# Sums of V and K rows in a decode step with its gradients: 64 one-column matmuls against 16 wide ones in column strips

## The chip, the cores and the metric

The kernel runs on one core of one Trainium2 chip. The metric is the device time of one execution in microseconds (us); the time of a kernel is the median over its runs. Engines are named as the profile names them: PE is TensorE's matmul and PEld its weight load, DVE is VectorE, ACT is ScalarE, POOL is GpSimd, SP is SyncE.

## What is computed

One token's residual step, x + attention + gated MLP on a layer-normed x, and its gradients with respect to x, the K and V caches and all weights. There are 32 heads, each with its own K and V cache of 8192 rows of 128 in bf16, so a cache of a head is 2 MB. Cut to attention:

```python
q = (xn @ wq) per head
scores = einsum("bhqd,bhkd->bhqk", q, k) * (Dh ** -0.5)
p = softmax(scores)
o = einsum("bhqk,bhkd->bhqd", p, v)
out = x + o_of_all_heads @ wo + mlp(xn)
# gradients, with do = the part of grad_out @ wo.T that belongs to the head
#   dv[k,:] = p[k] * do                  dp[k] = do . v[k,:]
#   u[k]    = p[k] * (dp[k] - sum(p*dp))
#   dk[k,:] = u[k] * scale * q           dq = scale * sum_k u[k] * k[k,:]
#   dwq, dwo, dx follow from dq, o and xn
```

Nearly all bytes are the caches read (2 x 64 MB) and the gradients dk and dv written (2 x 64 MB).

## The kernel before, in words

Setup (L102 to L665) loads and differentiates the MLP, while the first K and V tiles arrive. Then one loop over the heads (L691 to L741) follows, and a last head and an end (L743 on). All five engines' orders are written out by hand: an engine runs its instructions in the order of the program text, and each waits where its data aren't there yet.

A head's cache tile is 128 partitions x 64 row groups (j) x 128 columns (`Kt`, `Vt`). In the loop `c` is the current head and `n` the next. The next head's scores and its products with V are computed while the current head's gradients are written. For one head the steps are:

- `product` (L381): VectorE multiplies half the columns of K by q (or of V by do) into a tile `T` (L395), and TensorE adds these up with eight matmuls by the identity, of 512 moving columns each (L397), into the PSUM bank `psS` or `psDP`. Two halves make one product.
- `row_max` (L436): VectorE sums the bank into `S_sb` (L438) and takes the maximum (L440); TensorE brings the maxima of all partitions together (L442). `exps` (L445): VectorE's `negM` (L447), ScalarE's Exp (L450), TensorE's total (L451). `probs` (L453): VectorE's `rZ` (L455) and `P2` (L457), every probability twice, in bf16.
- `attend` (L462): o, the sum over rows of p times V. For each of the 64 row groups TensorE loads the group's 128x128 block of V as weights and multiplies it with one column of `P2`; all 64 add up in column 0 of the bank `ob` (L465).
- `row_dots` (L470) and `dscores` (L478): VectorE sums `psDP` (L472), its dot with P (L475), TensorE's total (L476), VectorE's `U2` (L480) and `Uf` (L485). Then dq in the same way as o: 64 weight loads of K blocks, 64 one-column matmuls into column 1 of `ob` (L487).
- `outer` (L400): dv and dk, half a head at a time, into `ot`: VectorE makes 24 of 32 row groups (L417), ScalarE eight (L411). A finished `ot` of 2 MB is stored by POOL's DMA queue (L424). Loads of K and V go by SP's queue (L112, L119).
- `turn_wq` and `keep_wq` (L490, L495) turn the head's part of wq. `weights` (L499): VectorE scales the two sums into `odq` (L502) and copies dq as bf16 (L504); ScalarE makes `dq_diag` (L506) and `om` (L510); TensorE spreads dq (L508), puts o in place for dwo (L513, a product with 32 weight columns whose output starts at partition 0, 32, 64 or 96) and adds to dx (L516). `keep_dq` (L519) keeps the spread dq.
- Once in four heads `prep_steps` (L271) prepares q and do for the next group of four, with copies `woT` by ScalarE (L288), and `finish_steps` (L335) writes dwo and, once in two groups, the columns of dwq. `gap()` places one such step at a time.

The columns of dwq that are done are stored in two pieces of three and two column blocks (`WQ_PARTS`, L428), both by `sparing` (L141): this splits a transfer of 128 partitions in 120 and 8 rows, and with small pad transfers into `lane_pad` (L134) sets which of the 16 DMA engines gets less of it.

In the loop VectorE's order around a head's end is: T of V second half (n), `odq` and `odq_bf` (c), T of K first half of the head after. TensorE's is: psDP second half (n), then `weights(c)`, then psS first half of the head after.

Of the kernel before, what the change touches and what calls it, by code (L numbers as in the profile page):

```python
# [9 lines left out]
BF16 = mybir.dt.bfloat16  # L10
F32 = mybir.dt.float32
ALU = mybir.AluOpType
ACTF = mybir.ActivationFunctionType
AX = mybir.AxisListType
PSUM = bass.MemoryType.PSUM

P = 128
# [4 lines left out]
def kernel(  # L22
# [22 lines left out]
    nc = tc.nc  # L45
# [16 lines left out]
    NB = NF + 1  # L62
    ACT_J = 8
    TAIL = 2
    LANES = 16
    SPARED = 4
    assert H % GW == 0 and GW % GH == 0 and 0 < REST < P and P % GH == 0
# [32 lines left out]
    with tc.manual_schedule(engines=ORDERED):  # L100
# [119 lines left out]
        DXN0 = 0  # L220
        OUT0 = NC
        OP0 = 16

        sel = consts.tile([P, P // GH], F32, name="sel")
        nc.vector.tensor_reduce(sel[:], ident_f[:].rearrange("p (q r) -> p q r", r=GH), AX.X, ALU.add)
        rmask = consts.tile([P, GH], F32, name="rmask")
        nc.vector.tensor_reduce(rmask[:], ident_f[:].rearrange("p (q r) -> p r q", r=GH), AX.X, ALU.add)

# [42 lines left out]
        def prep_steps(g):  # L271
            G_ = grp[g]
            wq_g, wo_g = G_["wq"], G_["wo"]

            def bank(name, dt, pool=None, tag="w"):
                if g == 0 and pool is not None:
                    return pool.tile([P, GH * DH], dt, name=name, tag=tag)
                return ps_w.tile([P, GH * DH], dt, name=name, tag="w")

            def turn(ci):  # L280
                ps_t = bank("ps_t", BF16, ps_o, "ob")
                for hh in range(GH):
                    nc.tensor.transpose(ps_t[:, hh * DH:(hh + 1) * DH], wo_g[:, hh, ci * P:(ci + 1) * P], ident_bf[:])  # L283
                return ps_t

            def keep(ps_t):
                woT = wpool.tile([P, GH * DH], BF16, name="woT", tag="woT", bufs=2)
                nc.scalar.copy(woT[:], ps_t[:])  # L288
                return woT

            ps_q = bank("ps_q", F32, ps_s, "sm")
            for ci in range(NC):
                nc.tensor.matmul(ps_q[:], lhsT=xn_col_bf[:, ci:ci + 1].to_broadcast([P, P]), rhs=wq_g[:, ci, :],
                                 start=(ci == 0), stop=(ci == NC - 1))
            yield
            qs_g = wpool.tile([P, GH, DH], BF16, name="qs_g", tag="qs_g")
            nc.scalar.activation(qs_g[:].rearrange("p h d -> p (h d)"), ps_q[:], ACTF.Copy, scale=scale)
            G_["qs"] = qs_g
            ps_t = turn(0)
            yield  # L300
            woT = keep(ps_t)
            ps_t = turn(1)
            yield
            ps_d = bank("ps_d", F32, ps_acc, "acc")
            for ci in range(NC):
                nc.tensor.matmul(ps_d[:], lhsT=g_col_bf[:, ci:ci + 1].to_broadcast([P, P]), rhs=woT[:], start=(ci == 0), stop=(ci == NC - 1))
                if ci + 1 < NC:
                    woT = keep(ps_t)
                if ci + 2 < NC:
                    ps_t = turn(ci + 2)  # L310
                if ci not in (2, NC - 1):
                    yield
            do_g = wpool.tile([P, GH, DH], BF16, name="do_g", tag="do_g")
            nc.scalar.copy(do_g[:].rearrange("p h d -> p (h d)").rearrange("p (q r) -> p r q", r=GH),  # L314
                           ps_d[:].rearrange("p (r q) -> p r q", r=GH))
            G_["do"] = do_g
# [108 lines left out]
                if columns:  # L425
                    store_columns()

        WQ_PARTS = ((0, 3), (3, 2))  # L428
        columns = []

        def store_columns():
            b, c0, n = columns.pop(0)
            part, _, dst = wq_part(b, c0, n)
            store(dst, part, by=sparing)

        def row_max(st):  # L436
            st.S = small.tile([P, J], F32, name="S_sb", bufs=1)
# [15 lines left out]
        def probs(st):  # L453
# [5 lines left out]
            nc.scalar.activation(st.Pf[:], st.E[:].rearrange("p (a j) -> p a j", a=2)[:, :, JH - ACT_J:JH],  # L459
                                 ACTF.Copy, scale=rZ[:])  # L460

        def attend(st):  # L462
            st.ob = ps_o.tile([P, 512], F32, name="ob", tag="ob")
            for j in range(J):
                nc.tensor.matmul(st.ob[:, 0:1], lhsT=st.V[:, j, :], rhs=st.P2[:, j, 0:1], start=(j == 0),  # L465
                                 stop=(j == J - 1), skip_group_check=True)
            while behind_o:
                on_sums(*behind_o.pop(0))

        def row_dots(st):  # L470
            st.DP = small.tile([P, J], F32, name="DP_sb", bufs=1)
            nc.vector.tensor_reduce(st.DP[:], st.ps["DP"][:], AX.X, ALU.add)  # L472
            rdot = small.tile([P, 1], F32, name="rdot")
            junk = small.tile([P, J], F32, name="junk", bufs=1)
            nc.vector.scalar_tensor_tensor(junk[:], st.DP[:], 1.0, st.P2[:, :, 0], ALU.mult, ALU.mult, accum_out=rdot[:])  # L475
            nc.tensor.matmul(st.sm[:, 4:5], lhsT=ones_f, rhs=rdot[:], start=True, stop=True, skip_group_check=True)  # L476

        def dscores(st):  # L478
            st.U2 = small.tile([P, J, 2], BF16, name="U2", bufs=1)
            nc.vector.scalar_tensor_tensor(st.U2[:], st.DP[:].unsqueeze(2).to_broadcast([P, J, 2]), st.sm[:, 4:5], st.P2[:],  # L480
                                           ALU.subtract, ALU.mult)
            st.Uf = None
            if st.h < H - 1:
                st.Uf = small.tile([P, 2, ACT_J], F32, name="Uf")
                nc.vector.tensor_copy(st.Uf[:], st.U2[:, :, 0].rearrange("p (a j) -> p a j", a=2)[:, :, JH - ACT_J:JH])  # L485
            for j in range(J):
                nc.tensor.matmul(st.ob[:, 1:2], lhsT=st.K[:, j, :], rhs=st.U2[:, j, 0:1], start=(j == 0), stop=(j == J - 1),  # L487
                                 skip_group_check=True)

        def turn_wq(st):  # L490
            st.ps_wqT = ps_w.tile([P, D], BF16, name="ps_wqT", tag="w")
# [6 lines left out]

        def weights(st):  # L499
            G_, hh = st.G, st.hh  # L500
            odq = small.tile([P, 2], F32, name="odq")
            nc.vector.tensor_tensor(odq[:], st.ob[:, 0:2], sc2[:], ALU.mult)  # L502
            odq_bf = small.tile([P, 1], BF16, name="odq_bf")
            nc.vector.tensor_copy(odq_bf[:], odq[:, 1:2])  # L504
            dq_diag = small.tile([P, P], BF16, name="dq_diag", bufs=1)
            nc.scalar.activation(dq_diag[:], ident_bf[:], ACTF.Copy, scale=odq[:, 1:2])  # L506
            st.ps_db = ps_w.tile([P, DH], F32, name="ps_db", tag="w")
            nc.tensor.matmul(st.ps_db[:], lhsT=ones_bf[:], rhs=dq_diag[:], start=True, stop=True)  # L508
            om = small.tile([P, GH], F32, name="om")
            nc.scalar.activation(om[:], rmask[:], ACTF.Copy, scale=odq[:, 0:1])  # L510
            if hh == 0:
                G_["on_ps"] = accbank[:, OP0 + GH * (st.g % 2):OP0 + GH * (st.g % 2 + 1)]
            nc.tensor.matmul(G_["on_ps"][hh * (P // GH):(hh + 1) * (P // GH), :], lhsT=sel[:], rhs=om[:],  # L513
                             start=True, stop=True, skip_group_check=True)
            for ci in range(NC):
                nc.tensor.matmul(accbank[:, DXN0 + ci:DXN0 + ci + 1], lhsT=st.wqT[:, ci * P:(ci + 1) * P],  # L516
                                 rhs=odq_bf[:], start=False, stop=True, skip_group_check=True)
# [75 lines left out]

        sm_f = wpool.tile([P, 9, NB], F32, name="sm_f", tag="dqbc_g", bufs=1)
        gate, up, th, sig, silu, hcol, t1, dgate, dup = (sm_f[:, i, :] for i in range(9))
        dhc = small.tile([P, NB], F32, name="dhc", bufs=1)
        dgu2 = small.tile([P, 2, NB], BF16, name="dgu2", bufs=1)
        hcol_bf = small.tile([P, NB], BF16, name="hcol_bf", bufs=1)
        nc.vector.memset(sm_f[:, 0:2, NF:NB], 0.0)
        dh0 = dh_product(0, W2A)  # L600
        dh1 = dh_product(W2A, W2A)
# [67 lines left out]
        def gap():  # L669
            if steps and next(steps[0], "end") == "end":  # L670
                steps.pop(0)

        first = new_head(0)
        product(first, "S", 0)
        nc.vector.tensor_reduce(dxn_mlp[:], dx_ps[:], AX.X, ALU.add)
# [15 lines left out]
        for h in range(H - 1):  # L691
# [13 lines left out]
            if n:  # L705
                product(n, "S", 1)
            outer(c, c.do, c.P2, c.Pf, "V", h, 1)
            if h + 2 < H:
                load_v(h + 2)
            wq_columns(h, 0)  # L710
# [1 line left out]
                load_wo(g + 1, nc.scalar)  # L712
            gap()
            dscores(c)
            outer(c, c.q, c.U2, c.Uf, "K", h, 0)
            keep_wq(c)
            if n:
                row_max(n)
                product(n, "DP", 0)
# [28 lines left out]
        outer(c, c.do, c.P2, None, "V", H - 1, 0)  # L748
        row_dots(c)
        outer(c, c.do, c.P2, c.Pf, "V", H - 1, 1)  # L750
        keep_dq(prev)
        while steps:
            gap()
        keep_wq(c)
        dscores(c)
        outer(c, c.q, c.U2, None, "K", H - 1, 0)
        weights(c)
        keep_dq(c)
# [33 lines left out]
            nc.sync.dma_start(out_1.rearrange("a b (p c) -> p (a b c)", c=NC), dx_bf[:])  # L792
        ps_fo = ps_w.tile([NC, P], F32, name="ps_o", tag="w")
        nc.tensor.transpose(ps_fo[:], fin[:], ident_f[:])
        fin_bf = consts.tile([NC, P], BF16, name="fin_bf")
        nc.vector.tensor_copy(fin_bf[:], ps_fo[:])
        nc.scalar.dma_start(out_0.rearrange("a b (c p) -> (a b c) p", p=P), fin_bf[:])

# [29 lines left out]
```

## Time and profile before

| | |
|---|---|
| median of three runs | 727.24 us (725.4 to 727.44) |
| the profiled execution's own time | 725.48 us |
| its span, first to last instruction | 723.5 us |
| mean granted TensorE clock | 0.789 of full speed |
| bytes moved by DMA | 303.72 MB, mean 420 GB/s |
| HBM read and written | 151.35 MB and 151.34 MB |
| `odq` (L502) of the first and of the last head | at 77.6 and 700.1 us |

A row of groups names line, engine, operation, output<-inputs, the form, the count, then busy time and mean time of one instruction, then the idle time of the engine just before them and what ended it. Consecutive matmuls overlap, so the busy time of a group is less than its count times the mean. A row of the timeline gives start, duration, engine, line, operation, tiles and count, and in brackets the idle time before it. An fp32 product stands as two weight loads and two matmuls. The granted clock moves between full and half speed within a head: eight psS or psDP matmuls take from 1.89 to 3.6 us.

### The profile page before, as it was taken

How to read it: one execution, taken by the hardware profiler on the slowest of the kernel's cores; microseconds unless marked ns; L12 is line 12 of the kernel's file. 1: busy time of each engine (PE TensorE's matmuls, PEld its weight loads, DVE VectorE, ACT ScalarE, POOL GpSimd, SP SyncE). 2: the span in 40 equal slices, each digit the busy share in tenths (PEclk: the TensorE clock that was granted, in tenths of full speed). 3: DMA queues.
4: the chain of work that ended last, by engine and by line, in shares of the span. 5: the costliest groups of instructions: out<-in, count | busy, mean ns of one | idle time of the engine just before them, and what ended most of it. 6: DMA issues, size and time to landing. Idle time of an engine off the chain costs nothing.

```text
span 723.5 us, 15790 instructions
## 1 busy us (share of the span) xinstructions
PE 555.5 (77%) x6513; PEld 324.3 (45%) x6513; DVE 630.3 (87%) x720; ACT 460.5 (64%) x1391; POOL 55.1 (8%) x98
## 2 busy tenths in 40 slices
PE   5778788778888787887788685778787878787860
PEld 3654444443544454443454342444354435444440
DVE  4789999899989996998899885899799988999990
ACT  2175666786568774785577653786667846787550
POOL 0010000000000210100000200010000000000100
PEclk9698988877877888787687888687788778877775
DMA  9999999999999999999999999999999999999996
GB/s 359 413 415 424 430 430 427 428 427 431 426 431 428 426 424 428 427 412 429 430 427 429 428 427 422 430 411 410 433 425 429 426 432 427 430 429 429 423 424 255
DMA packets 27142, 303.72 MB, mean 420 GB/s; under 512 B 3422, under 2 KB 3494, under 8 KB 9406
## 3 DMA queue, kind: packets, MB, share of 16 engines
q1 hardware_dynamic: 13778, 155.41, 50.9%
q0 software_dynamic: 11552, 139.43, 45.6%
q10 hardware_dynamic: 1740, 7.87, 2.6%
q8 instruction: 51, 0.84, 0.4%
q14 instruction: 21, 0.17, 0.1%
HBM read 151.35 MB, written 151.34 MB: 418 GB/s over the span
## 4 chain that ended last, share of the span: by engine, by line
DMA 42%; DVE 31%; PE 15%; ACT 7%; issue 1%; SPq 0%; POOL 0%; DVEq 0%; ACTq 0%; POOLq 0%
DMA out_dram<-ot 19%; DMA Kt<-in_A_k_cache_dram 15%; DVE T L395 15%; DVE ot L417 10%; PE psS L397 5%; ACT ot L411 4%; DMA lane_pad<-in_A_wq_dram 4%; PE ob L465 2%; DMA out_dram<-wo_g 2%; PE psDP L397 2%; DMA dbc<-in_B_w_dram 2%; DVE S_sb L438 1%; DVE DP_sb L472 1%; PE ob L487 1%; ACT do_g L314 1%
## 5 line engine op out<-in xcount | busy, mean ns | idle before, releaser
L397 PE MATMUL psDP<-T,ident_bf 128*128 128x512 bf16 x512 | 185.8, 529 | 58.7 <-DVE T L395 58.6
L397 PEld LDWEIGHTS <-ident_bf 128*128 128x128 bf16 x1024 | 121.3, 121 | 220.7 <-issue 170.5
L411 ACT ACTIVATE ot<-qs_g,Uf 128x128 bf16<-128x128 bf16 x496 | 151.4, 389 | 58.9 <-DMA out_dram<-wo_g 32.0
L411 ACT ACTIVATE ot<-do_g,Pf 128x128 bf16<-128x128 bf16 x504 | 153.9, 389 | 11.9 <-DMA out_dram<-ot 10.9
L395 DVE TENSOR_TENSOR T<-Kt,qs_g 128x4096 bf16<-128x4096 bf16 x64 | 146.5, 2288 | 16.4 <-DMA Kt<-in_A_k_cache_dram 15.4
L397 PE MATMUL psS<-T,ident_bf 128*128 128x512 bf16 x512 | 148.3, 442 | 6.2 <-DVE T L395 6.1
L395 DVE TENSOR_TENSOR T<-Vt,do_g 128x4096 bf16<-128x4096 bf16 x64 | 146.0, 2281 | 3.9 <-ACT do_g L314 3.7
L417 DVE TENSOR_TENSOR ot<-do_g,P 128x3072 bf16<-128x3072 bf16 (+1 forms) x64 | 112.8, 1763 | 13.7 <-DMA out_dram<-ot 12.7
L417 DVE TENSOR_TENSOR ot<-qs_g,U 128x3072 bf16<-128x3072 bf16 (+1 forms) x64 | 113.2, 1768 | 11.4 <-DMA out_dram<-ot 11.4
L424 POOL DMA_DIRECT2D out_dram<-ot x60 | 32.4, 539 | 534.2 <-DVE Uf L485 275.0
L487 PEld LDWEIGHTS <-Kt 128*128 128x128 bf16 x2048 | 57.5, 97 | 11.6 <-issue 8.9
L487 PE MATMUL ob<-U,Kt 128*128 128x1 bf16 x2048 | 56.8, 164 | 1.7 <-DVE U L480 1.5
L465 PEld LDWEIGHTS <-Vt 128*128 128x128 bf16 x2048 | 56.9, 98 | 0.0
L465 PE MATMUL ob<-P,Vt 128*128 128x1 bf16 x2048 | 56.1, 163 | 0.0
L506 ACT ACTIVATE dq_diag<-ident_bf,odq 128x128 bf16<-128x128 bf16 x32 | 12.8, 400 | 42.3 <-DVE odq L502 42.3
L459 ACT ACTIVATE Pf<-E,rZ 128x16 f32<-128x16 f32 x32 | 9.7, 304 | 45.0 <-DVE rZ L455 40.5
L288 ACT COPY woT<-ps_t 128x512 bf16<-128x512 bf16 x40 | 23.0, 576 | 17.8 <-PE ps_t L283 17.8
L283 PE MATMUL ps_t<-ident_bf,wo_g 128*128 128x128 bf16 x160 | 17.1, 234 | 19.6 <-ACT dqbc_g L523 15.0
L442 PE MATMUL sm<-ident_f,mrow 128*128 128x128 f32 x64 | 17.2, 355 | 18.6 <-DVE mrow L440 18.6
L438 DVE TENSOR_REDUCE S_sb<-psS 128x64 f32<-128x512 f32 x32 | 21.9, 685 | 8.1 <-PE psS L397 8.1
L283 PEld LDWEIGHTS <-wo_g 128*128 128x128 bf16 x160 | 13.6, 106 | 31.6 <-issue 28.4
L476 PE MATMUL sm<-rdot,ones_fc 128*128 128x1 f32 x64 | 11.3, 245 | 18.5 <-DVE junk L475 18.4
(160 smaller groups left out, 508.6 us busy)
## 6 DMA issues: line engine op xcount, KB each, us to landing
out_dram<-ot POOLq DMA_DIRECT2D x60, 2048.0 KB, 27.4
Kt<-in_A_k_cache_dram SPq DMA_DIRECT2D x32, 2048.0 KB, 27.2
Vt<-in_A_v_cache_dram SPq DMA_DIRECT2D x32, 2048.0 KB, 20.5
out_dram<-ot SPq DMA_DIRECT2D x8, 1024.0 KB, 16.5
out_dram<-wo_g ACTq DMA_DIRECT2D x6, 640.0 KB, 15.7
wo_g<-in_A_wo_dram ACTq DMA_DIRECT2D x6, 640.0 KB, 15.5
wq<-in_A_wq_dram SPq DMA_DIRECT2D x2, 1280.0 KB, 20.5
w1t<-in_B_w_dram SPq DMA_DIRECT2D x1, 2160.0 KB, 12.3
```

What stands on the lines that cost most here:

```text
L283: nc.tensor.transpose(ps_t[:, hh * DH:(hh + 1) * DH], wo_g[:, hh, ci * P:(ci + 1) * P], ident_bf[:])
L288: nc.scalar.copy(woT[:], ps_t[:])
L395: nc.vector.tensor_tensor(T[:], src[:, :, ds_], vec[:, ds_].unsqueeze(1).to_broadcast([P, J, DHH]), ALU.mult)
L397: nc.tensor.matmul(ps[:], lhsT=ident_bf[:], rhs=T[:, :, RUN * i:RUN * (i + 1)], start=(half == 0 and i == 0), stop=(half == 1 and i == DHH ...
L411: nc.scalar.activation(st.ot[half][:, JH - ACT_J + j].rearrange("p a b -> p (a b)"), vec, ACTF.Copy, scale=wf[:, half, j:j + 1])
L417: nc.vector.tensor_tensor(st.ot[half][:, 0:n], vec.rearrange("p (a b) -> p a b", b=2).unsqueeze(1).to_broadcast([P, n, DH // 2, 2]), w2[:, ...
L424: nc.gpsimd.dma_start(dst.rearrange("p j d -> p (j d)"), st.rows[:])
L438: nc.vector.tensor_reduce(st.S[:], st.ps["S"][:], AX.X, ALU.add)
L442: nc.tensor.matmul(st.sm[:, 8:8 + P], lhsT=mrow[:].to_broadcast([P, P]), rhs=ident_f[:], start=True, stop=True, skip_group_check=True)
L465: nc.tensor.matmul(st.ob[:, 0:1], lhsT=st.V[:, j, :], rhs=st.P2[:, j, 0:1], start=(j == 0), stop=(j == J - 1), skip_group_check=True)
L487: nc.tensor.matmul(st.ob[:, 1:2], lhsT=st.K[:, j, :], rhs=st.U2[:, j, 0:1], start=(j == 0), stop=(j == J - 1), skip_group_check=True)
L506: nc.scalar.activation(dq_diag[:], ident_bf[:], ACTF.Copy, scale=odq[:, 1:2])
```

## The change

The sums o and dq are made the other way round. Four row groups at a time, the four columns of `P2` (or `U2`) are the weights and the 4 x 128 columns of V (or K) move: 16 matmuls with 4 weight columns and 512 moving columns. Number q writes four partitions from 32 x (q mod 4) on, so the sixteen go round four strips of the array, and each strip adds up four of them. A strip's partition s then holds, in its block s of 128 columns, a part of the sum; the other blocks hold products that aren't wanted. ScalarE copies the whole bank `ob` to SBUF in two halves (`keep_rows`, fp32, in the buffers of `woT`, of which there are now three), and four fp32 matmuls with one moving column (`blocks_sum`) pick block r of the strips with a 0/1 column of `pick` and add up to the column `od`, which `odq` reads in place of `ob`. `ob` is zeroed once, so the 112 partitions that no matmul writes hold zeros.

```diff
+        def wide_sums(src, w2):
+            n = J // WIDE
+            for q in range(n):
+                c0 = STRIP * (q % NS)
+                nc.tensor.matmul(ob[c0:c0 + WIDE, :], lhsT=w2[:, WIDE * q:WIDE * (q + 1), 0],
+                                 rhs=src[:, WIDE * q:WIDE * (q + 1), :].rearrange("p j d -> p (j d)"),
+                                 start=(q < NS), stop=(q >= n - NS), skip_group_check=True)
+        def keep_rows(st):
+            st.wide = []
+            for i in range(2):
+                part = wpool.tile([P, WIDE // 2 * DH], F32, name="wide", tag="woT", bufs=3)
+                nc.scalar.copy(part[:], ob[:, i * (WIDE // 2) * DH:(i + 1) * (WIDE // 2) * DH])
+                st.wide.append(part)
+        def blocks_sum(st, k):
+            c0 = OD0 + 2 * (st.h % 2)
+            st.od = accbank[:, c0:c0 + 2]
+            for r in range(WIDE):
+                i, b = divmod(r, WIDE // 2)
+                nc.tensor.matmul(st.od[:, k:k + 1], lhsT=st.wide[i][:, b * DH:(b + 1) * DH], rhs=pick[:, r:r + 1],
+                                 start=(r == 0), stop=(r == WIDE - 1), skip_group_check=True)
         def attend(st):
-            st.ob = ps_o.tile([P, 512], F32, name="ob", tag="ob")
-            for j in range(J):
-                nc.tensor.matmul(st.ob[:, 0:1], lhsT=st.V[:, j, :], rhs=st.P2[:, j, 0:1], start=(j == 0),
-                                 stop=(j == J - 1), skip_group_check=True)
+            wide_sums(st.V, st.P2)
...
         def dscores(st):
-            for j in range(J):
-                nc.tensor.matmul(st.ob[:, 1:2], lhsT=st.K[:, j, :], rhs=st.U2[:, j, 0:1], start=(j == 0), stop=(j == J - 1),
-                                 skip_group_check=True)
+            wide_sums(st.K, st.U2)
...
         def weights(st):
             G_, hh = st.G, st.hh
+            blocks_sum(st, 1)
             odq = small.tile([P, 2], F32, name="odq")
-            nc.vector.tensor_tensor(odq[:], st.ob[:, 0:2], sc2[:], ALU.mult)
+            nc.vector.tensor_tensor(odq[:], st.od, sc2[:], ALU.mult)
...
+        ob = ps_o.tile([P, 512], F32, name="ob", tag="ob")
+        nc.tensor.matmul(ob[:], lhsT=ident_bf[:], rhs=zero_bf[:].to_broadcast([P, WIDE * DH]), start=True, stop=True)
...
             outer(c, c.do, c.P2, c.Pf, "V", h, 1)
+            keep_rows(c)
...
             dscores(c)
+            blocks_sum(c, 0)
             outer(c, c.q, c.U2, c.Uf, "K", h, 0)
             keep_wq(c)
+            keep_rows(c)
...
```

So `blocks_sum(c, 0)`, for o, stands behind the K sums on TensorE, and `blocks_sum(c, 1)`, for dq, at the head of `weights`, behind psDP's second half. The last head has the same four calls.

Beside this, the second piece of the dwq columns is stored by one plain DMA instead of `sparing`:

```diff
-        WQ_PARTS = ((0, 3), (3, 2))
+        WQ_PARTS = ((0, 3, sparing), (3, 2, nc.gpsimd.dma_start))
```

To make room in SBUF `junk` is written over `S_sb`, and four small tiles of the setup and the end (`dhc`, `dgu2`, `hcol_bf`, `fin_bf`) share buffers with others. `pick` and `zero_bf` are made in the setup.

More of the change, by code (lines that the diff above doesn't have):

```diff
@@ L64 @@
     TAIL = 2
+    STRIP = 32
+    NS = P // STRIP
+    WIDE = 4
     LANES = 16
@@ L222 @@
         OP0 = 16
+        OD0 = 32
         sel = consts.tile([P, P // GH], F32, name="sel")
         nc.vector.tensor_reduce(sel[:], ident_f[:].rearrange("p (q r) -> p q r", r=GH), AX.X, ALU.add)
+        pick = consts.tile([P, WIDE], F32, name="pick")
+        nc.vector.tensor_reduce(pick[:], ident_f[:].rearrange("p (c s) -> p s c", s=STRIP)[:, 0:WIDE, :], AX.X, ALU.add)
+        zero_bf = consts.tile([P, 1], BF16, name="zero_bf")
+        nc.vector.memset(zero_bf[:], 0.0)
         rmask = consts.tile([P, GH], F32, name="rmask")
@@ L286, in keep @@
             def keep(ps_t):
-                woT = wpool.tile([P, GH * DH], BF16, name="woT", tag="woT", bufs=2)
+                woT = wpool.tile([P, GH * DH], BF16, name="woT", tag="woT", bufs=3)
                 nc.scalar.copy(woT[:], ps_t[:])
@@ L426, in outer_v @@
                     store_columns()
-        WQ_PARTS = ((0, 3), (3, 2))
+        WQ_PARTS = ((0, 3, sparing), (3, 2, nc.gpsimd.dma_start))
         columns = []
         def store_columns():
-            b, c0, n = columns.pop(0)
+            b, c0, n, by = columns.pop(0)
             part, _, dst = wq_part(b, c0, n)
-            store(dst, part, by=sparing)
+            store(dst, part, by=by)
         def row_max(st):
@@ L473, in row_dots @@
             rdot = small.tile([P, 1], F32, name="rdot")
-            junk = small.tile([P, J], F32, name="junk", bufs=1)
-            nc.vector.scalar_tensor_tensor(junk[:], st.DP[:], 1.0, st.P2[:, :, 0], ALU.mult, ALU.mult, accum_out=rdot[:])
+            nc.vector.scalar_tensor_tensor(st.S[:], st.DP[:], 1.0, st.P2[:, :, 0], ALU.mult, ALU.mult, accum_out=rdot[:])
             nc.tensor.matmul(st.sm[:, 4:5], lhsT=ones_f, rhs=rdot[:], start=True, stop=True, skip_group_check=True)
@@ L595 @@
         gate, up, th, sig, silu, hcol, t1, dgate, dup = (sm_f[:, i, :] for i in range(9))
-        dhc = small.tile([P, NB], F32, name="dhc", bufs=1)
-        dgu2 = small.tile([P, 2, NB], BF16, name="dgu2", bufs=1)
-        hcol_bf = small.tile([P, NB], BF16, name="hcol_bf", bufs=1)
+        dhc = small.tile([P, NB], F32, name="dhc", tag="Pf")
+        dgu2 = small.tile([P, 2, NB], BF16, name="dgu2", tag="Pf")
+        hcol_bf = small.tile([P, NB], BF16, name="hcol_bf", tag="Uf")
         nc.vector.memset(sm_f[:, 0:2, NF:NB], 0.0)
@@ L750 @@
         outer(c, c.do, c.P2, c.Pf, "V", H - 1, 1)
+        keep_rows(c)
         keep_dq(prev)
@@ L755 @@
         dscores(c)
+        blocks_sum(c, 0)
+        keep_rows(c)
         outer(c, c.q, c.U2, None, "K", H - 1, 0)
@@ L794 @@
         nc.tensor.transpose(ps_fo[:], fin[:], ident_f[:])
-        fin_bf = consts.tile([NC, P], BF16, name="fin_bf")
+        fin_bf = small.tile([NC, P], BF16, name="fin_bf", tag="dq_diag", bufs=1)
         nc.vector.tensor_copy(fin_bf[:], ps_fo[:])
```

## The prediction

> **What bounds the kernel now.** I read the page's parts 1 and 2 first, then the busy time by stage, then who VectorE waits for, then the order of time around one head's end.
>
> ```profile
> PE 555.5 (77%) x6513; PEld 324.3 (45%) x6513; DVE 630.3 (87%) x720; ACT 460.5 (64%) x1391; POOL 55.1 (8%) x98
> PEclk9698988877877888787687888687788778877775
> DMA  9999999999999999999999999999999999999996
> ```
>
> The 16 DMA engines are full nearly throughout, and VectorE is busy 87%. Both limit the kernel, in turn. The next view cuts the main loop from the first head's `odq` (L502, 77.61 us) to the 31st head's (691.88); each row gives the stretch, its length and VectorE's busy time, TensorE's granted clock, the DMA share and GB/s.
>
> ```profile
> 77.61:96.34 18.73, 18.45 (x22) 0.84 1.01 431
> 77.61:691.88 614.27, 556.39 (x601) 0.79 1.01 427
> 700.07:723.47 23.40, 5.51 (x19) 0.50 0.71 294
> ```
>
> A head in which VectorE waits for nobody lasts 18.73 us. Many later heads last 18.74 as well, but the mean of the 30 is 614.27 / 30 = 20.48. What fills the other 1.74 us a head, 52.2 us in all, is in VectorE's waits (total, times, longest):
>
> ```profile
> DVE ot L417 <- DMA out_dram<-ot: 24.0, 8, 8.1
> DVE T L395 <- DMA Kt<-in_A_k_cache_dram: 15.4, 8, 4.3
> DVE S_sb L438 <- PE psS L397: 8.1, 9, 2.8
> DVE T L395 <- ACT do_g L314: 3.7, 5, 0.8
> DVE T L395 <- PE psDP L397: 0.9, 1, 0.9
> ```
>
> 39.4 us are waits for transfers (for a store to free `ot`, for K to land), 12.7 for TensorE and ScalarE. So VectorE could bear about 39.4 / 30 = 1.3 us more a head: only transfers' time would be taken. Beyond that each added microsecond lengthens the kernel 30 times.
>
> **Where the change adds a wait.** The end of head 0, in order of time:
>
> ```profile
> 75.41 2.28 DVE L395 TENSOR_TENSOR T<-Vt,do_g 128x4096 bf16<-128x4096 bf16 x1
> 77.61 0.15 DVE L502 TENSOR_TENSOR odq<-ob,sc 128x2 f32<-128x2 f32 x1
> 77.74 1.89 PE L397 MATMUL psDP<-T,ident_bf 128*128 128x512 bf16 x8 [0.55 <-DVE T L395]
> 77.87 2.29 DVE L395 TENSOR_TENSOR T<-Kt,qs_g 128x4096 bf16<-128x4096 bf16 x1
> ```
>
> `odq` follows VectorE's last T at once, since `ob` was ready long before, and the next head's T follows `odq`. TensorE can begin its eight psDP matmuls only when that T ends. In the changed program `odq` reads what `blocks_sum(1)` writes, and its four products stand in TensorE's queue behind those eight matmuls; VectorE's order is unchanged: T, `odq`, `odq_bf`, next T. So VectorE stands still for the eight matmuls and the four products, in every head. Queued behind the waiting `odq` is all of VectorE's next head, and TensorE, ScalarE and the stores wait for that.
>
> **The parts and their costs.** The groups (busy us, mean ns of one; idle before):
>
> ```profile
> L487 PE MATMUL ob<-U,Kt 128*128 128x1 bf16 x2048 | 56.8, 164 | 1.7 <-DVE U L480 1.5
> L465 PE MATMUL ob<-P,Vt 128*128 128x1 bf16 x2048 | 56.1, 163 | 0.0
> L476 PEld LDWEIGHTS sm<-rdot,ones_fc 128*128 128x128 f32 x64 | 11.1, 199 | 30.3 <-DVE junk L475 27.9 <-issue 1.4
> L513 PEld LDWEIGHTS accbank<-om,sel 128*32 128x32 f32 x64 | 4.7, 114 | 11.2 <-issue 9.7 <-ACT om L510 1.2 <-ACT wq L353 0.3
> L288 ACT COPY woT<-ps_t 128x512 bf16<-128x512 bf16 x40 | 23.0, 576 | 17.8 <-PE ps_t L283 17.8
> L523 ACT CAST dqbc_g<-ps_db 128x128 bf16<-128x128 f32 x32 | 7.8, 242 | 0.2 <-PE ps_db L508 0.2
> ```
>
> *psDP ahead of `odq`.* Eight matmuls take 1.89 us at the fast clock and about 3.5 at the slow one (3.57 at 192.40). Over the 31 heads they end 1.94 us after T in the median; without the five heads that start over a microsecond late the mean is 2.3, which I take. Bounds 1.94 and 3.6.
>
> *blocks_sum.* One fp32 product is two weight loads and two matmuls (64 of each for 32 at L476). Two loads start 0.11 us apart at the fast clock (475.85, 475.96) and 0.21 at the slow. Four products are eight loads and a last matmul of 0.25: 8 x 0.11 + 0.25 = 1.1 us, slow 2.0; if they packed better than any row shows, still one product's 0.38. I take 1.1: dense work stands just before. `blocks_sum(0)` costs as much, but lies in the 3 us that TensorE's L442 finishes ahead of VectorE's `negM`.
>
> **Added stall: 2.3 + 1.1 = 3.4 us a head**, bounds 2.3 and 5.6.
>
> *The sums.* Removed: 64 matmuls in 56.1 / 32 = 1.75 us, twice a head. Added: 16 matmuls of 512 columns, each 1.89 / 8 = 0.236 us. No row shows strips side by side. Bounds: all four at once, 4 x 0.236 = 0.95 us; one by one, 3.8. I take 1.75, no change, between them. In heads with the fast clock psS ends 1.78 us before VectorE reads it, which covers a longer V sum; with the slow clock only 0.04 to 0.6, and there it delays L438 one for one.
>
> The Trainium skill ("TensorEngine Tiling (Array Packing)", Key Properties) says that tiles run matmuls in parallel, which speaks for the 0.95, and that a change of tiling mode drains TensorE, which speaks against the change. The one strip product here, L513, agrees with the drain: 9.7 us of idle "issue" ahead of 30 weight loads, 0.32 each; two changes around the V sum would be 0.6 us, by which the sum stays as it is in fast heads and grows by some 10 us if half the heads have no cover.
>
> *keep_rows.* Four ScalarE copies of 128x256 a head; between the 242 ns of 128 columns and the 576 of 512, about 0.35 us each: 1.4 us a head, 45 us in all, on an engine that is 36% idle. The V pair follows the last V scaling and is done before TensorE reaches the K sums. The K pair sits ahead of the second K scaling; its second copy also needs a third `woT` buffer, so it waits for `blocks_sum(0)`. Exp then waits for `negM` as now. Without cover it is about 1 us in the heads that scale `wo_g` there, some 8 us. ScalarE's own DMA issues (wo loads and stores) come later by the same, under 20 us of landing time.
>
> *The unspared columns.* POOL issues four DMAs fewer (94 for 98, at 0.5 to 0.9 us); POOL is 8% busy: nothing. SP's order is the same. *Setup*: `pick`, the zeroing matmul and shared buffers lie in waits for the first loads: nothing.
>
> **Sum.** First `odq` 77.6 + 3.4 = 81.0. Thirty heads of 18.74 + 3.4 = 22.14: 664.2. Of the 12.7 us of TensorE and ScalarE waits I keep half, as the stall lets them catch up: 6.4. The waits for transfers go: 303.7 MB at 427 GB/s is 711 us of work within a longer loop. Last head 8.2 + 1.5 (no psDP there; K sums, copies and products outlast the one `ot` of 2.29): 9.7. The tail from the last `odq` is now 23.4 us, of which the calculation takes 6.4; the rest drains stores. With the queues emptied in the loop it should need about 12. The profiled execution was 725.48 for a span of 723.5: 2.0. Together 81.0 + 664.2 + 6.4 + 9.7 + 12 + 2.0 = 775.3; the median of the runs before, 727.24, is 1.8 above the profiled one, so I say **776**.
>
> **Rivals.**
> 1. *The strips run one by one.* V sum 2.05 longer against 1.78 of cover: 0.25; K sum, products and L442 take 3.8 + 1.1 + 0.4 = 5.3 where VectorE has 4.8 until `negM`: 0.5. 0.75 x 31 = 23 us: 799 (with dense work the clock should be fast; where it isn't, more). For: no row shows overlap. Against: the four outputs lie in separate strips. 0.20.
> 2. *The clock is slow in the stall.* 3.6 + 2.0 = 5.6, that is 2.2 more x 31 = 68: 844. For: PEclk averages 0.79. Against: psDP's second half, after the first, is mostly fast already. 0.07.
> 3. *Other side: transfers go on setting the pace.* Decided by the stall: under 1.3 us a head VectorE only loses waits for transfers. Then fewer instruction fetches show: 8192 weight loads and matmuls go, 2048 + 1024 come, 5120 x 64 bytes (0.84 MB of queue 8 over 13026) = 0.33 MB; spread, 0.8 us; if all on one of 16 engines at 427 / 16 GB/s, 12 us of that engine. Time 713 to 725, say 718. For: the DMA row. Against: even the fast psDP alone is 1.89. 0.03.
> 4. *The change doesn't cost what it seems to:* the sums shrink, but `odq` waits only for part of this (stall about 2): 20.7 a head, 730 to 740. 0.04.
>
> **Numbers.** Forecast (750 to 792 with its bounds) 0.66; rivals as above. A measurement tells about 0.3% from no change. Faster 0.03, within 0.3% 0.01, slower 0.96. The range takes in the forecast's bounds and rival 1: 748 to 815.
>
> **What would show it.** VectorE's waits led by `odq` <- PE accbank (L491 products), about 3.4 us x 31 = 105 us; `odq` to `odq` near 22.3 us; DMA waits of VectorE under 10 us; DMA share near 0.93; wide sums of 1 to 2 us each. Wrong if `odq` shows no wait, if heads still take 20.5 us, or if L438 waits over 1 us in most heads.

## The result and the profile after

The changed kernel takes 776.5 us (median of four runs, 774.59 to 779.52), the kernel before 726.87: a ratio of 1.069, 95% interval 1.0644 to 1.0735. The forecast was 776 in a range of 748 to 815. The profiled execution took 774.59 us for a span of 772.8. The ratios leave out a run that is more than 1.5% above the fastest of its kernel; here that is one run, the 749.48 us under **Later `odq`**.

First the same rows of the page's parts 1 and 2:

```profile
PE 597.4 (77%) x3954; PEld 310.1 (40%) x3954; DVE 630.2 (82%) x722; ACT 496.5 (64%) x1519; POOL 52.2 (7%) x94
PEclk9698788778896788777897688867887788867785
DMA  8999989999999999999999999999999999999974
GB/s 352 419 423 427 429 338 397 389 374 391 409 396 367 410 409 432 425 370 431 426 411 383 406 394 432 425 380 424 428 417 380 391 393 397 397 363 378 399 307 182
```

VectorE's work is the same to 0.1 us (630.2 for 630.3), its share of the longer span is smaller, and the bytes per second have fallen well below 427 in many slices: the transfers no longer set the pace. (The tenths of the DMA row hide this; the GB/s row shows it. The same bytes took more of the engines' time: a share of 0.99 for 399 GB/s in the loop below, where it was 1.01 for 427.) Now the loop, from the first `odq` to the second, to the 31st, and the tail after the last:

```profile
80.23:101.86 21.63, 18.59 (x21) 0.76 1.01 429
80.23:744.64 664.41, 556.05 (x601) 0.79 0.99 399
756.06:772.80 16.74, 5.50 (x18) 0.50 0.40 148
```

Thirty heads take 664.41 us, 22.15 each, against 20.48 before. VectorE's waits show what fills the difference:

```profile
DVE odq L529 <- PE accbank L491: 106.6, 32, 4.3
DVE sm_f L589 <- PE gate_ps L584: 3.8, 1, 3.8
DVE S_sb L447 <- PE psS L406: 2.0, 1, 2.0
```

The wait at `odq`, absent before, is 106.6 us in 32 heads, 3.33 each. The waits for transfers, 39.4 us before, are gone from the list, and so are those for TensorE and ScalarE: in the thirty heads `odq` is VectorE's only wait (the other two rows stand before the first `odq`). The place itself, at the end of head 0:

```profile
74.42 2.28 DVE L404 TENSOR_TENSOR T<-Vt,do_g 128x4096 bf16<-128x4096 bf16 x1
76.75 2.66 PE L406 MATMUL psDP<-T,ident_bf 128*128 128x512 bf16 x8 [0.28 <-DVE T L404]
79.25 0.95 PE L491 MATMUL accbank<-pick,wide 128*128 128x1 f32 x8
80.23 0.16 DVE L529 TENSOR_TENSOR odq<-accbank,sc 128x2 f32<-128x2 f32 x1 [3.54 <-PE accbank L491]
80.50 2.28 DVE L404 TENSOR_TENSOR T<-Kt,qs_g 128x4096 bf16<-128x4096 bf16 x1
```

T ends at 76.70; TensorE does the eight psDP matmuls, then the four products (eight passes), and only then does `odq` run, with the next head's T behind it. Before, `odq` stood at 77.61, right after T.

The new operations by themselves:

```profile
L475 PE MATMUL ob<-Vt,P 128*4 128x512 bf16 x512 | 42.6, 464 | 0.0
L475 PE MATMUL ob<-Kt,U 128*4 128x512 bf16 x512 | 34.0, 386 | 1.4 <-DVE U L508 1.3
L491 PE MATMUL accbank<-pick,wide 128*128 128x1 f32 x512 | 70.9, 260 | 0.0
L483 ACT COPY wide<-ob 128x256 f32<-128x256 f32 x128 | 40.5, 366 | 6.8 <-PE ob L475 6.2 <-PE accbank L491 0.6
```

A V sum takes 42.6 / 32 = 1.33 us, a K sum 34.0 / 32 = 1.06, against 1.75 before. So the sums did become quicker, by 36 us of TensorE's time in all, but the products that pick their blocks take 70.9.

### The profile page after: what moved, and what is told of

Same layout as the page of the kernel before. It is cut to its first block, busy times and chain, and to the rows that moved or that the text cites. A ratio compares the mean times of both kernels' runs of the same rounds, so it can differ in the third digit from the quotient of the medians.

```text
span 772.8 us, 10896 instructions
## 1 busy us (share of the span) xinstructions
PE 597.4 (77%) x3954; PEld 310.1 (40%) x3954; DVE 630.2 (82%) x722; ACT 496.5 (64%) x1519; POOL 52.2 (7%) x94
## 4 chain that ended last, share of the span: by engine, by line
DVE 68%; PE 19%; ACT 5%; DMA 4%; issue 2%; SPq 0%; DVEq 0%; ACTq 0%
DVE T L404 32%; DVE ot L426 23%; PE psDP L406 11%; PE accbank L491 4%; ACT ot L420 4%; DVE S_sb L447 2%; DVE DP_sb L501 2%; DMA out_dram<-wo_g 2%; DMA dbc<-in_B_w_dram 2%; DVE P L466 1%; DVE U L508 1%; PE psS L406 1%; DVE S_sb L503 1%; ACT wo_g L352 1%; DVE odq L529 1%
## 5 line engine op out<-in xcount | busy, mean ns | idle before, releaser
L406 PE MATMUL psDP<-T,ident_bf 128*128 128x512 bf16 x512 | 166.5, 484 | 69.0 <-DVE T L404 69.0
L406 PE MATMUL psS<-T,ident_bf 128*128 128x512 bf16 x512 | 162.9, 475 | 31.4 <-DVE T L404 31.4
L529 DVE TENSOR_TENSOR odq<-accbank,sc 128x2 f32<-128x2 f32 x32 | 5.1, 159 | 106.6 <-PE accbank L491 106.6
L491 PEld LDWEIGHTS accbank<-pick,wide 128*128 128x128 f32 x512 | 72.4, 211 | 20.4 <-issue 16.3
L491 PE MATMUL accbank<-pick,wide 128*128 128x1 f32 x512 | 70.9, 260 | 0.0
L483 ACT COPY wide<-ob 128x256 f32<-128x256 f32 x128 | 40.5, 366 | 6.8 <-PE ob L475 6.2
L475 PE MATMUL ob<-Vt,P 128*4 128x512 bf16 x512 | 42.6, 464 | 0.0
L475 PE MATMUL ob<-Kt,U 128*4 128x512 bf16 x512 | 34.0, 386 | 1.4 <-DVE U L508 1.3
L535 PE MATMUL ps_db<-dq_diag,ones_bf 128*128 128x128 bf16 x32 | 7.3, 228 | 22.4 <-ACT dq_diag L533 22.4
L504 PEld LDWEIGHTS sm<-rdot,ones_fc 128*128 128x128 f32 x64 | 17.2, 286 | 14.8 <-DVE S_sb L503 12.1
## 6 DMA issues: line engine op xcount, KB each, us to landing
out_dram<-wo_g ACTq DMA_DIRECT2D x6, 640.0 KB, 13.4
w1t<-in_B_w_dram SPq DMA_DIRECT2D x1, 2160.0 KB, 12.3
```

The source lines that it names most:

```text
L406: nc.tensor.matmul(ps[:], lhsT=ident_bf[:], rhs=T[:, :, RUN * i:RUN * (i + 1)], start=(half == 0 and i == 0), stop=(half == 1 and i == DHH ...
L475: nc.tensor.matmul(ob[c0:c0 + WIDE, :], lhsT=w2[:, WIDE * q:WIDE * (q + 1), 0], rhs=src[:, WIDE * q:WIDE * (q + 1), :].rearrange("p j d -> ...
L483: nc.scalar.copy(part[:], ob[:, i * (WIDE // 2) * DH:(i + 1) * (WIDE // 2) * DH])
L491: nc.tensor.matmul(st.od[:, k:k + 1], lhsT=st.wide[i][:, b * DH:(b + 1) * DH], rhs=pick[:, r:r + 1], start=(r == 0), stop=(r == WIDE - 1), ...
```

## The experiments

The theory is that the cost is a position: `odq` waits behind psDP's second half and the four products. The rivals are that the new work itself costs the time, that the strips don't run side by side, and that the plain store of two columns matters. Each time stands with the ratio to the kernel before, run beside it on the same chip.

**Early products.** The four products for dq go ahead of psDP's second half (in the last head, which has none, they stay just before `odq`); all else of the change stays.

```diff
             outer(c, c.q, c.U2, c.Uf, "K", h, 1)
+            blocks_sum(c, 1)
...
         def weights(st):
-            blocks_sum(st, 1)
```

> The changed kernel with one edit: the four block products for dq stand ahead of psDP's second half on TensorE instead of behind it; the sums, the copies, the unspared columns and VectorE's order stay. Wait theory (VectorE stands at odq for psDP's second half and the products): the products now run in TensorE's idle time before VectorE's last T ends, so odq no longer waits, VectorE's 106.6 us at odq go, heads of 18.74 us come back and transfers set the pace again: 718 to 728 us. Rival (the wide sums, the four fp32 copies or the fp32 products cost the time by themselves, wherever they stand): it stays above 745 us.

Measured: 724.65 us, ratio 0.9977 (0.9964 to 0.9989). VectorE's waits in it:

```profile
DVE odq L528 <- PE accbank L491: 24.9, 26, 3.1
DVE ot L426 <- DMA out_dram<-ot: 17.1, 7, 7.7
DVE T L404 <- DMA Kt<-in_A_k_cache_dram: 7.7, 5, 2.6
```

Moving four small matmuls takes back all of the 50 us and a little more: the wide sums, the copies and the products, still all there, cost nothing at this place. Waits for transfers are back, 24.8 us of the 39.4. Of the 24.9 us left at `odq`, 15.6 come in 14 heads where psDP's first half ran at the slow clock (3.57 us) and 3.1 in the last head. In the loop what is left is some 0.7 us a head, under the 1.3 that the prediction said VectorE could bear. One of the 14 heads:

```profile
314.95 2.04 PEld L491 LDWEIGHTS accbank<-pick,wide 128*128 128x128 f32 x8 [0.28 <-ACT wo_g L352]
315.37 1.70 PE L491 MATMUL accbank<-pick,wide 128*128 128x1 f32 x8
317.18 0.16 DVE L528 TENSOR_TENSOR odq<-accbank,sc 128x2 f32<-128x2 f32 x1 [1.16 <-PE accbank L491]
```

The eight loads take 2.04 us there, where they take 0.97 or 1.08 at the fast clock.

**The old sums, late.** The kernel before, with its 64 one-column matmuls for dq moved to the head of `weights`, behind psDP's second half. Nothing of the new work is in it.

```diff
         def dscores(st):
...
-            for j in range(J):
-                nc.tensor.matmul(st.ob[:, 1:2], lhsT=st.K[:, j, :], rhs=st.U2[:, j, 0:1], ...)
...
         def weights(st):
             G_, hh = st.G, st.hh
+            for j in range(J):
+                nc.tensor.matmul(st.ob[:, 1:2], lhsT=st.K[:, j, :], rhs=st.U2[:, j, 0:1], ...)
```

> The kernel before with one edit: its 64 one-column matmuls for dq stand behind psDP's second half, where the changed kernel has its products; no wide sums, no copies. Wait theory: odq waits 2.3 + 1.75 = 4.05 us in each of 31 heads, so a head lasts 18.74 + 4.05 = 22.8 us and the kernel some 785 to 800 us. Rival (the new work itself is the cost): little changes, 727 to 740 us.

Measured: 807.9 us, ratio 1.112 (1.1103 to 1.1136).

```profile
DVE odq L502 <- PE ob L499: 135.3, 31, 5.3
DVE S_sb L438 <- PE psS L397: 7.1, 9, 2.0
```

The position alone, with the old work in it, makes the old kernel slower than the changed one. The wait is 135.3 / 31 = 4.36 us a head, not 4.05: here psDP's second half took over 2.2 us in 21 of 31 heads, against 16 in the kernel before, at a mean granted clock of 0.74 in the profiled run. With that the time lies 8 us above the expected range; the direction and the place are as expected.

**One strip.** The changed kernel with all sixteen matmuls of a sum in strip 0.

```diff
-                c0 = STRIP * (q % NS)
+                c0 = 0
-                                 start=(q < NS), stop=(q >= n - NS), ...
+                                 start=(q == 0), stop=(q == n - 1), ...
```

> The changed kernel with one edit: all sixteen wide matmuls of a sum write the same strip (partitions 0 to 3) instead of going round four; the result is the same. If the strips run side by side, a sum of now 1.03 us takes 16 x 0.236 = 3.8 us; the V sum is then 2.75 us longer where psS ended some 1.5 us before VectorE read it, so about 1.2 us more a head at L447: 800 to 820 us. If consecutive matmuls merely follow each other closely and the strips do nothing, 774 to 780 us as before.

Measured: 818.01 us, ratio 1.1257 (1.123 to 1.1283).

```profile
L475 PE MATMUL ob<-Vt,P 128*4 128x512 bf16 x512 | 119.7, 388 | 0.0
L475 PE MATMUL ob<-Kt,U 128*4 128x512 bf16 x512 | 115.7, 379 | 0.6 <-DVE U L508 0.6
```

A V sum now takes 119.7 / 32 = 3.74 us, a K sum 115.7 / 32 = 3.62. VectorE's wait for psS rose from 2.0 to 25.0 us and the one at `odq` from 106.6 to 113.8; with three smaller ones its waits explain about 38 of the 45 us between the two profiled executions, and 5 more are VectorE's own busy time (635.6 us for 630.2). So the strips do run side by side: the same sixteen matmuls in four strips took 1.03 us at the fast clock. That settles the first rival of the prediction. Its price of 799 was too low: it took 1.78 us of cover for the V sum, but in nearly all heads of the changed kernel psS ends only 1.2 to 1.5 us ahead of VectorE's read, and the longer wait at `odq` was not in it.

**Later `odq`.** The changed kernel with `odq` and what follows moved behind the next head's first T, the products left where the change put them: 2.29 us of VectorE's work then covers the wait.

```diff
             if n:
                 product(n, "DP", 1)
-            weights(c)
+            blocks_sum(c, 1)
...
                 product(n, "S", 0)
+            if prev:
+                weights(prev)
```

> The changed kernel with one edit: the block products stay behind psDP's second half, but VectorE's odq (and what hangs on it) comes after the next head's first T, so 2.29 us of VectorE's work covers the wait. Wait theory with the point of decision: the stalls of 3.7, 2.8, 2.8 and 4.4 us become 1.4, 0.5, 0.5 and 2.1, 1.1 in the mean, which is under the 1.3 us that waits for transfers leave: 724 to 735 us. Rival (the stall counts in full, no slack): 18.74 + 1.1 a head on top of the old mean of 20.48, 755 to 765 us.

Measured: 746.48 us (737.12 to 749.48), ratio 1.023 (1.018 to 1.0279). This is between the two expectations and was met by neither. The runs lie far apart, and the profile is of the quickest alone, at 737.12; why the others took 8 to 12 us more is not known. In it:

```profile
DVE odq L528 <- PE accbank L491: 46.9, 25, 5.6
DVE T L404 <- DMA Kt<-in_A_k_cache_dram: 16.7, 10, 4.4
```

The stall left is 46.9 us, 1.5 a head, not 1.1, and 16.7 us of waits for K still stand beside it. The two failures of the estimate: the stall was larger, and the waits for transfers were not all there to be used up. Of the 16.7 us, 13.4 fall in five heads that wait at `odq` for 0.3 us in all, so a stall in one head did not use up a late transfer in another. By the point of decision, 1.5 for 1.3 us a head should cost 0.2 x 30 = 6 us; even this run lost 11. In this kernel the 1.3 us is thus an upper bound of what can be hidden.

**Both cures.** Products early and `odq` later.

> Both cures: early block products and odq behind the next head's first T. The 24.9 us that VectorE still waited at odq with early products go. If transfers set the pace, that only becomes waits for transfers, 722 to 725 us; if the stalls still cost in heads that don't wait for transfers, up to 24 us go at most, but not below the transfers' floor: 716 to 722 us.

Measured: 724.45 us, ratio 0.9974 (0.996 to 0.9988), the same as early products alone.

```profile
DVE ot L426 <- DMA out_dram<-ot: 22.3, 12, 5.5
DVE T L404 <- DMA Kt<-in_A_k_cache_dram: 10.2, 7, 3.2
DVE S_sb L447 <- PE psS L406: 4.3, 4, 2.0
DVE DP_sb L501 <- PE psDP L406: 3.9, 7, 1.1
...
DVE odq L528 <- PE accbank L491: 3.1, 1, 3.1
```

The wait at `odq` is gone but for the last head's, and the time did not move. Of the 21.8 us that the loop's waits at `odq` took, 8.4 came back as waits for transfers (33.2 us for 24.8), as expected, and some 11 as waits for TensorE and ScalarE at other places (12.3 us for 1.3), which was not expected. The loop's rate is 426 GB/s with and without the later `odq`, which fits transfers that set the pace; that they alone held the time is not shown.

**The unspared columns.** The kernel before with only the plain store of the second piece; then with both pieces plain; and the kernel with early products with both spared, and with both plain.

```diff
-        WQ_PARTS = ((0, 3), (3, 2))
+        WQ_PARTS = ((0, 3, sparing), (3, 2, nc.gpsimd.dma_start))
```

> The kernel before with only the second piece of the dwq columns stored by one plain DMA. Theory: not on any path that ends last, 725 to 729 us. Rival (one DMA engine that also fetches instructions gets 2 x 512 KB / 16 = 64 KB more, 2.4 us at 427/16 GB/s, and is the last): 729 to 731 us.

> The kernel before with both pieces of the dwq columns stored by plain DMAs. Theory of the one engine: beside the 64 KB of the second piece (2.6 us measured) it gets 2 x 768 KB / 16 = 96 KB more, 3.7 us at 427/16 GB/s: 726.3 + 2.6 + 3.7 = 732 to 733 us. If the plain store of the second piece cost time by its moment or by POOL's order, the first piece need not cost anything: 728 to 730 us.

> The kernel with early products (724.65 us) with one edit: both pieces of the dwq columns spared again. Theory of the one engine (it fetches instructions and ends last; the plain store cost 2.6 us in the kernel before, against 2.4 from 64 KB at 427/16 GB/s): if it still ends last with 0.33 MB of fetches fewer, 2 us faster, 722 to 723.5. If the fewer fetches have brought it level with the others, no change, 724 to 725.5. Rival (the plain store in the kernel before cost time by its moment, not by its engine): 2 us or more either way with no such bound.

> The kernel with early block products with both pieces unspared. Theory of the one engine: it fetches 0.33 MB less, 12 us of its time, more than the 6.3 us of both pieces, so it is not the last: no change, 724 to 725.5 us. If the cured kernel were as near the edge as the one before, 3.7 us slower: 728 us.

> As the one before with both pieces of the dwq columns spared. Same difference to it as the spared kernel with early products has to the unspared one: 2 us faster if one engine ends last, else none.

| kernel | pieces plain | us | ratio to before (95%) |
|---|---|---|---|
| before, one piece plain | second | 729.08 | 1.0035 (1.0022 to 1.0047) |
| before, both plain | both | 732.68 | 1.0095 (1.0079 to 1.011) |
| early products | none | 724.19 | 0.9976 (0.996 to 0.9993) |
| early products (as above) | second | 724.65 | 0.9977 (0.9964 to 0.9989) |
| early products | both | 726.87 | 1.0007 (0.9997 to 1.0017) |
| both cures | none | 724.59 | 0.9977 (0.996 to 0.9994) |

In the kernel before, the plain store of the second piece costs 0.35% or 2.6 us, and both pieces 0.95% or 6.6 us, close to the 2.5 and 6.1 us that one engine would need for 64 and 160 KB more at a sixteenth of 427 GB/s. That is what the engine spared before gets more; the others get a little less. My own theory for the first of these runs, no effect, fell (by 0.08 us of its range, but the ratio's interval lies above 1); the rival's price was met. With 0.33 MB of instruction fetches fewer (the page's queue 8 went from 51 packets and 0.84 MB to 31 and 0.51) the second piece costs nothing to be seen, and both together 0.3%, some 2 us. That fits one engine that fetches instructions and ends last, but the two kernels differ in more than the fetches, and an engine that is last for another reason is not ruled out. And both pieces plain were expected to cost nothing there, and did cost; so if there is such an engine, its room is smaller than the 12 us of all the fetches saved. Which engine it is, and how the fetches lie on the engines, the trace does not show, and it stays open.

## Why the prediction was right, point by point

- **What bounds the kernel.** Right. A head without waits is 18.74 us in VectorE's order and the transfers fill most of the rest; a stall beyond the transfers' slack counts in every head. The late old sums show this without the new work, the early products show the new work without most of the stall. A slip: of the 12.7 us of waits for TensorE and ScalarE, 2.9 stand before the first `odq`, so the thirty heads had 9.8.
- **The added stall, 3.4 us.** Measured 3.33. It differs by head and repeats every four: about 2.8, 2.8, 4.3 and 3.7 us. In the higher two psDP's second half took 2.7 us instead of 1.89, and in the 4.3 the products took 1.71 instead of 0.95. Products elsewhere: 0.95 to 1.05 us at the fast clock, close to the 1.1 priced. A slip in the working: in the kernel before, the median from T's end to psDP's end is 2.30 us, and 1.94 is the shortest; the 2.3 that was taken, a mean, is right.
- **The sums.** Bounds right, size off: 1.33 and 1.06 us where 1.75 was taken, near the bound of four at once. On VectorE's path it made no difference, as said. The Trainium skill's rule that tiles run in parallel ("TensorEngine Tiling (Array Packing)", Key Properties) is borne out: 3.62 us in one strip against 1.03 in four at the fast clock, a factor of 3.5. Behind a wide sum the weight loads stand idle for 0.44 us, which would fit the same section's drain, but the next matmul begins 0.06 us before the sum ends (308.81 and 308.87, by the profile's modelled ends), so it costs nothing here; no run shows what the idle time is.
- **keep_rows.** Four copies at 366 ns, 40.5 us in all, hidden, as priced (0.35 each).
- **The thirty heads.** 664.41 measured, 664.2 from 18.74 + 3.4. The further 6.4 us of TensorE and ScalarE waits that I kept did not come: none was left in these heads. The stall gave the other engines time to catch up fully, not by half.
- **The signs.** All came but one: a DMA share near 0.93 was expected, and it is 0.99. The rate did fall to 399 / 427 = 0.93; that the share falls with the rate was wrong.
- **The end.** The last head took 11.4 us (744.64 to 756.06) for 9.7 expected: both sets of products stand before its `odq`, at the slow clock, 3.57 us for the sixteen passes. The tail is 16.7 us for 12: the calculation ends 6.2 us after the last `odq`, and 10.5 us follow, at a DMA share of 0.33. So the queues were nearly empty as said, but the last small transfers have a time of their own (6.4 us from issue to landing for `dx_bf`); what fills the other 4 us is not shown. These two, 6.4 us too little, and the loop, forecast at 670.6 us and so 6.2 too much, cancel; that the total came within a microsecond is luck to that extent. The sum also gives 775.3 for the profiled execution (774.59), and with the 1.8 us to the median 777.1, not the 776 that was said. The steps that carry it, 664 of 772 us, were right by themselves.
- **The unspared columns cost nothing.** No run spares them in the changed kernel itself. That they cost nothing there fits the total, since transfers don't set its pace, but the reason was wrong: POOL's time was the wrong thing to price. In the kernel before, whose pace transfers do set, the same edit costs 2.6 us.

## What to carry to other kernels

Before replacing an operation by a faster one, look at where its result is read: an engine in order stands still for all that its releaser has queued ahead. Here 50 us hung on four small matmuls placed behind eight others; placed ahead of them, the same work takes 0.23% less than the old kernel (0.11 to 0.36). And in a kernel bound by transfers try which way a store is split: a plain one here cost what one engine needs for its extra share, though why that engine should end last stays open.

## What the runs showed of the hardware that was not expected

- Four column strips with four weight columns each and 512 moving columns ran 3.5 times as fast as one strip (1.03 against 3.62 us for sixteen, at the fast clock).
- In the kernel before, 64 KB more on the one engine that `sparing` had spared cost 2.6 us and 160 KB cost 6.6, as if one engine alone set the end, though the mean DMA share stood at 1.01 in the loop.
- The DMA share is no measure of what the engines could still move: it was 0.99 at 399 GB/s and 1.01 at 427.
- In the one-strip run, with TensorE denser (83% busy against 77%), the mean granted clock rose from 0.789 to 0.915, and the kernel was slower all the same.
